# Which ten queries share a block of the attention: neighbours in the score tile, or every twelfth

## The chip, the core and the metric

The kernel runs on one core of a Trainium2 chip. Its time is the device time of one execution in microseconds (us), and a kernel's time is the median over its runs. The core has TensorE (PE in the profile, with its weight loads as PEld), VectorE (DVE), ScalarE (ACT), GpSimd (POOL) and SyncE (SP). SP computes nothing here; it issues nearly all transfers, which 16 DMA engines carry out.

## What is computed

The reference is an attention with mixed heads, followed by a mixture of experts of which each token takes one:

```python
scores = scale * np.matmul(q, k.transpose(0, 1, 3, 2))    # q, k, v: (8, 12, 448, 64)
scores = np.einsum('bhij,hg->bgij', scores, w_pre)        # the 12 heads are mixed
scores = scores - np.max(scores, axis=-1, keepdims=True)
attn = np.exp(scores)
attn = attn / (np.sum(attn, axis=-1, keepdims=True) + 1e-09)
attn = np.einsum('bhij,hg->bgij', attn, w_post)           # and mixed again
attn_out = np.matmul(attn, v)
...
x = np.ascontiguousarray(attn_out.transpose(0, 2, 1, 3)).reshape(B * S, H * D)   # 3584 x 768
expert_idx = np.argmax(x @ w_gate, axis=1)                # one of 8 experts for each token
h = np.maximum(xe @ w1[e], 0.0)
out[mask] = gate_w[mask, None] * (h @ w2[e])
```

## The kernel before

**Tiles.** Each of the 8 batches has 448 queries, cut into four tiles of 120, 120, 120 and 88 queries; so there are 32 tiles T. For a tile, `qk` (L187) multiplies queries by keys, two heads at a time, into PSUM with the query on the partition; ScalarE and VectorE copy the two heads (L200, L201) into the score tile `si`, which holds [query, head, key]: one partition for a query, 12 x 448 numbers in it. There are two such tiles in turn.

**Blocks and halves.** Mixing the heads is a matmul that contracts over the heads, so the heads have to lie on partitions. A tile's queries are therefore cut into blocks of 20, and a block into two halves of 10: `geom[T][3]` (L50 to L55) lists the sizes of the halves. A tile of 120 has 6 blocks; a tile of 88 has 4 blocks and one that is a single half of 8. `relayout` (L207) moves a half by one DMA from 10 partitions of `si` to 120 partitions of a buffer `sb`, row 4 + 12 i + h for query i and head h, 448 numbers (1792 bytes) for each. There are four buffers `sb`, each with room for two halves. Both DMAs of a block are issued from SP at L212.

**Work on a block.** `mix` (L215) multiplies each half by a block-diagonal 124 x 124 matrix (L222, into `bm`), takes the row maximum on VectorE (L223) and the exponential with its sum on ScalarE (L224, into `et`). `weigh` (L229) makes the reciprocal of the sums and scales the second mixing matrix with it on GpSimd (L237, into `wp`). `post` (L241) multiplies `et` by `wp`, which mixes the heads again and turns the block so that keys lie on partitions (L248, into `bp`), and copies each half into the tile `pt` [112 keys, 4, head, 120 queries] at the places of its queries (L254: the first half on ScalarE, the second on VectorE). `av` (L258) multiplies by the values (L267), `rows` (L274), `choose` and `dispatch` send a token's row to HBM (XD) and place it in its expert's list.

**The order.** The attention's order is written out by hand (L416 to L434) and every engine keeps to it. For block u it is: the two DMAs of `relayout` of block u + 2, then `mix` of u, `post` of u - 2, `weigh` of u, then what the table `after` has for that block. For a tile's third block (slot 2) this is `values` of the tile before and `scores` (the six `qk`) of the tile after. So between the last score of the next tile and the first `mix` of that tile lie blocks 3, 4, 5 of a tile with six blocks, but block 3 and the half block 4 of a tile with five. SP takes its DMAs strictly in this order: the queries' loads (L100, two DMAs, at a tile's last but one block), the keys' loads (L84), the values' load (L115) and the stores of XD (L288) stand between the relayouts. A DMA into `sb` waits until the `mix` that read that buffer is done; the first of a tile waits for the last copy into `si`.

**After the attention** come the experts (L446 to L582), matmuls over weights that are loaded and split as they go, and a loop for the rest, which the change does not touch.

Of the kernel before, what the change touches and what calls it, by code (L numbers as in the profile page):

```python
# [19 lines left out]
B, H, S, D = 8, 12, 448, 64  # L20
# [5 lines left out]
IB = 10  # L26
NB = 2 * IB
IQ = 5
R0, R1 = 4, 124
# [11 lines left out]
def attn_moe_kernel(ctx, tc, qT, kT, v, w_pre, w_post, w_gate, w1, w2, out):  # L41
    nc = tc.nc
# [4 lines left out]
    XD = dram.tile([NT, HD], F32, name="XD")  # L47
    TB = dram.tile([ROWS, 2], F32, name="TB")

    geom = []  # L50
    for T in range(NTILE):
        it = T % 4
        ni = min(IT, S - it * IT)
        geom.append((T // 4, it, ni, [[min(IB, ni - i) for i in range(s, min(s + NB, ni), IB)]
                                      for s in range(0, ni, NB)]))  # L55


    kq = ctx.enter_context(ExitStack())
# [19 lines left out]
    KR, KK, QR, QQ, VV, SI, SB, EE, PT, XT = ({} for _ in range(10))  # L78
# [14 lines left out]
        KK[b, c] = (kh, kl)  # L93

    def load_q(T):
        b, it, ni, _ = geom[T]
        qr = q_p.tile([P, NPAIR, IT], F32, name="qr")
        src = qT[b, :, H * it * IT:H * (it * IT + ni)].rearrange("d (c t i) -> t d c i", c=NPAIR, t=2)
        for half in range(2):
            nc.sync.dma_start(out=qr[half * D:(half + 1) * D, :, :ni], in_=src[half])  # L100
        QR[T] = qr
# [25 lines left out]
    for c in range(4):  # L127
# [19 lines left out]
        out=Wpre[:, R0:].rearrange("p (i g) -> p i g", g=H),  # L147
# [13 lines left out]
    for c in range(NPAIR):  # L161
# [22 lines left out]
                        in_=none.unsqueeze(1).to_broadcast([P, 8, ROWS // P // 8, 2]))  # L184


    def qk(T, c):  # L187
        b, it, ni, _ = geom[T]
        if c == 0:
            SI[T] = si_p.tile([IT, H, S], F32, name="si")  # L190
        kh, kl = KK[b, c]
        qh, ql = QQ[T]

        bs = bank_s[c % 2]
        for n, (qx, kx) in enumerate(((qh, kh), (qh, kl), (ql, kh))):
            for r in range(2):
                hs = slice(r * D, (r + 1) * D)
                nc.tensor.matmul(out=bs[:ni, r, :S], lhsT=qx[hs, c, :ni], rhs=kx[hs, :],  # L198
                                 start=(n == 0), stop=(n == 2))
        nc.scalar.copy(out=SI[T][:ni, 2 * c, :], in_=bs[:ni, 0, :S])  # L200
        nc.vector.tensor_copy(out=SI[T][:ni, 2 * c + 1, :], in_=bs[:ni, 1, :S])  # L201
# [5 lines left out]
    def relayout(T, s):  # L207
        sb = sbs[nsb["n"] % len(sbs)]
        nsb["n"] += 1
        for c, nq in enumerate(geom[T][3][s]):  # L210
            q0 = s * NB + c * IB
            nc.sync.dma_start(out=sb[R0:R0 + nq * H, c, :], in_=SI[T][q0:q0 + nq])  # L212
        SB[T, s] = sb

    def mix(T, s):  # L215
# [25 lines left out]
    def post(T, s):  # L241
        if s == 0:
            PT[T] = pt_p.tile([JC, NJ, H, IT], F32, name="pt")
        et, wp = EE.pop((T, s))
        for n, nq in enumerate(geom[T][3][s]):
            pp = bank_p[n]
            for c in range(NJ):
                nc.tensor.matmul(out=pp[:, c * IT:(c + 1) * IT],  # L248
                                 lhsT=et[:R1, n, c * JC:(c + 1) * JC],
                                 rhs=wp[:R1, n, :], start=True, stop=True)  # L250
        for n, nq in enumerate(geom[T][3][s]):
            i0 = s * NB + n * IB
            copy = (nc.scalar.copy, nc.vector.tensor_copy)[n]
            copy(out=PT[T][:, :, :, i0:i0 + nq].rearrange("p c h i -> p (c h) i"),  # L254
                 in_=bank_p[n][:, :NJ * IT].rearrange("p (x i) -> p x i", i=IB)[:, :, :nq])


    def av(T, g):  # L258
        b, it, ni, _ = geom[T]
        if g == 0:  # L260
            XT[T] = x_p.tile([P, NPAIR, IT], F32, name="xt")
        pa = bank_s[g][:, 0, :3 * IT].rearrange("p (c i) -> p c i", i=IT)
        for p in range(3):
            for c in range(NJ):
                for r in range(2):
                    h = 2 * (3 * g + p) + r
                    nc.tensor.matmul(out=pa[r * D:(r + 1) * D, p, :ni],  # L267
                                     lhsT=VV[b][:, c, h * D:(h + 1) * D],
                                     rhs=PT[T][:, c, h, :ni], start=(c == 0), stop=(c == NJ - 1))
        nc.vector.tensor_copy(out=XT[T][:, 3 * g:3 * g + 3, :ni], in_=pa[:, :, :ni])  # L270
# [1 line left out]
    XR, LG = {}, {}  # L272

    def rows(T, part):  # L274
        b, it, ni, _ = geom[T]
        if part == 0:
            XR[T] = x_p.tile([IT, NPAIR, P], F32, name="xr", bufs=1)
            LG[T] = sm_p.tile([IT, 2, NE], F32, name="lg")
        pxv = bank_s[part][:, 0, :3 * XG].rearrange("p (c x) -> p c x", x=XG)
        for c in range(3):  # L280
            nc.tensor.matmul(out=pxv[:ni, c, :], lhsT=XT[T][:, part * 3 + c, :ni],
                             rhs=xg[:, part * 3 + c, :], start=True, stop=True)
        nc.scalar.copy(out=XR[T][:ni, part * 3:part * 3 + 3, :], in_=pxv[:ni, :, :P])
        nc.vector.reduce_sum(out=LG[T][:ni, part, :],
                             in_=pxv[:ni, :, P:XG].rearrange("p c e -> p e c"), axis=AX.X)
        if part == 1:
            t0 = b * S + it * IT
            nc.sync.dma_start(out=XD[t0:t0 + ni, :],  # L288
                              in_=XR.pop(T)[:ni].rearrange("p c x -> p (c x)"))
# [2 lines left out]


    def choose(T):
        b, it, ni, _ = geom[T]
        lg2 = LG.pop(T)
        lg = sm_p.tile([IT, NE], F32, name="lgs")
        nc.vector.tensor_add(out=lg[:ni], in0=lg2[:ni, 0, :], in1=lg2[:ni, 1, :])
        m8 = sm_p.tile([IT, NE], F32, name="m8")
        i8 = sm_p.tile([IT, NE], U32, name="i8")  # L300
        nc.vector.max(out=m8[:ni], in_=lg[:ni])
        nc.vector.max_index(out=i8[:ni], in_max=m8[:ni], in_values=lg[:ni])
        sc = sm_p.tile([IT, 4], F32, name="sc")
        nc.vector.tensor_copy(out=sc[:ni, 0:1], in_=i8[:ni, 0:1])
        ohb = sm_p.tile([IT, NE], BF16, name="ohb")
        nc.vector.tensor_scalar(out=ohb[:ni], in0=iota8[:ni], scalar1=sc[:ni, 0:1], scalar2=None,
                                op0=ALU.is_equal)
        nc.vector.tensor_scalar(out=sc[:ni, 1:2], in0=m8[:ni, 0:1], scalar1=-1.0, scalar2=None,
                                op0=ALU.mult)
        ex = sm_p.tile([IT, NE], F32, name="ex")  # L310
        nc.scalar.activation(out=ex[:ni], in_=lg[:ni], func=AF.Exp, bias=sc[:ni, 1:2],
                             scale=1.0, accum_out=sc[:ni, 2:3])
        LG[T] = (sc, ohb)

    def dispatch(T):
        b, it, ni, _ = geom[T]
        sc, ohb = LG.pop(T)
        pr = bank_s[0][:, 1, :]
        nc.tensor.matmul(out=pr[:ni, 0:NE], lhsT=tri[:ni, :ni], rhs=ohb[:ni], start=True, stop=True)
        nc.tensor.matmul(out=pr[:, NE:2 * NE], lhsT=ones[:ni, :], rhs=ohb[:ni], start=True, stop=True)  # L320
        nc.vector.tensor_scalar(out=sc[:ni, 2:3], in0=sc[:ni, 2:3], scalar1=1e-9, scalar2=None,
                                op0=ALU.add)
        tg = sm_p.tile([IT, 2], F32, name="tg")
        nc.vector.reciprocal(out=tg[:ni, 1:2], in_=sc[:ni, 2:3])
        nc.vector.tensor_copy(out=tg[:ni, 0:1].bitcast(I32), in_=tokid[:ni, b, it:it + 1])
        pos = sm_p.tile([IT, NE], F32, name="pos")
        nc.vector.tensor_tensor(out=pos[:ni], in0=pr[:ni, 0:NE], in1=state["base"][:ni], op=ALU.add)
        nc.vector.tensor_tensor(out=pos[:ni], in0=pos[:ni], in1=ohb[:ni], op=ALU.mult)
        di = sm_p.tile([IT, 1], I32, name="di")
        nc.vector.reduce_sum(out=sc[:ni, 3:4], in_=pos[:ni], axis=AX.X)  # L330
        nc.vector.tensor_copy(out=di[:ni], in_=sc[:ni, 3:4])
        nc.gpsimd.indirect_dma_start(
            out=TB[:, :], out_offset=bass.IndirectOffsetOnAxis(ap=di[:ni, 0:1], axis=0),
            in_=tg[:ni, :], in_offset=None, bounds_check=ROWS - 1, oob_is_err=False)
        last = T == NTILE - 1
        nbase = (const if last else sm_p).tile([P, NE], F32, name="cbase" if last else "nbase")
        nc.vector.tensor_tensor(out=nbase, in0=pr[:, NE:2 * NE], in1=state["base"], op=ALU.add)
        state["base"] = nbase
# [38 lines left out]
        after.setdefault((T, s), []).append(what)  # L377

    for T in range(NTILE):
        b, it, ni, _ = geom[T]  # L380
        n = len(geom[T][3])
        last = T + 1 == NTILE
        if T + 2 < NTILE:
# [32 lines left out]
    for u in range(NU + PLAG):  # L416
# [6 lines left out]
        if u < NU:  # L423
# [3 lines left out]
            T, s = blocks[u]  # L427
# [7 lines left out]
    T = NTILE - 1  # L435
# [264 lines left out]
```

## Time and profile before

| what | value |
|---|---|
| median of 3 runs | 1793.27 us (1791.68 to 1803.64) |
| the profiled execution | 1798.46 us, span from first to last instruction 1796.7 us |
| attention, from the first score to the last token's row | about 7 to 1225 us of the span |
| experts | about 1225 to 1785 us |
| mean granted clock of TensorE over the span | 0.956 |
| L212 issues on SP, `sb<-si` | 352 DMAs of 210.0 KB and 8 of 168.0 KB |

How to read it: the page of the profile gives busy times by engine, then the costliest groups of instructions by line, with the idle time of the engine just before them and what ended that idle time (the releaser). The view of waits sums such idle times. The view of stretches gives each engine's busy time between two moments, the granted clock of TensorE (1.00 is full speed) and the share of the 16 DMA engines that was busy. The view of DMA queues gives packets, bytes and the share of the 16 engines' time that the packets took. In the timeline each row has the start in us, the duration, the engine, the line, the operation, output and inputs, the count, and in brackets the idle time before and its releaser.

### The profile page before, as it was taken

Reading aid. Unit: us, or ns where it says so; the run is one execution under the profiler, and the core shown is the slowest. Engines: PE = TensorE matmul, PEld = TensorE weight load, DVE = VectorE, ACT = ScalarE, POOL = GpSimd, SP = SyncE. Lnnn points to the kernel's source line nnn. Section 1 sums busy time; section 2 is a strip of 40 time slices with the busy share of each in tenths; the row PEclk is TensorE's granted clock in tenths of the full one; section 3 lists DMA queues with packets and bytes.
Section 4 is the critical chain, followed back from the end, with each engine's and each line's share of the span. In section 5 each row is a group of like instructions: output and inputs, shape, how many; then the busy total and the mean of one; then the engine's idle time right before and its main releaser. Section 6 shows DMA issues by size and latency. Waiting matters only on the chain. (4 is left out here: it accounts for less than half of the span.)

```text
span 1796.7 us, 29795 instructions
## 1 busy us (share of the span) xinstructions
PE 1538.0 (86%) x11056; PEld 1233.2 (69%) x11056; DVE 812.7 (45%) x2011; ACT 703.3 (39%) x1608; POOL 428.0 (24%) x595
## 2 busy tenths in 40 slices
PE   3788788788789788888879889965999999999996
PEld 1566566566566566666657666655988889898986
DVE  1455454455455545545445545543334333344330
ACT  2344444345345444444434544532324233234230
POOL 4224223123222322323312422212102102011000
PEclk9899999899899999989999999987999999999998
DMA  3554455355455455445535544444335244154220
GB/s 87 138 108 81 98 127 103 75 117 127 78 122 107 90 110 122 81 98 132 107 75 121 126 82 85 94 109 139 127 117 186 87 148 161 59 197 170 85 90 33
DMA packets 114468, 197.53 MB, mean 110 GB/s; under 512 B 39746, under 2 KB 88914, under 8 KB 114308
## 3 DMA queue, kind: packets, MB, share of 16 engines
q1 hardware_dynamic: 107200, 171.51, 40.1%
q0 software_dynamic: 6064, 23.86, 3.5%
q8 instruction: 100, 1.64, 0.4%
q14 instruction: 60, 0.49, 0.1%
q10 hardware_dynamic: 1044, 0.04, 0.0%
HBM read 96.01 MB, written 23.06 MB: 66 GB/s over the span
## 5 line engine op out<-in xcount | busy, mean ns | idle before, releaser
L222 PE MATMUL bm<-sb,Wpre 124*124 124x448 f32 x720 | 350.4, 596 | 150.8 <-DMA sb<-si 114.8
L248 PEld LDWEIGHTS bp<-wp,et 124*112 124x112 f32 x2880 | 349.4, 189 | 87.6 <-issue 84.2
L237 POOL TENSOR_SCALAR wp<-Wpost,st 124x120 f32<-124x120 f32 x360 | 206.2, 584 | 831.4 <-DVE st L234 733.7
L248 PE MATMUL bp<-wp,et 124*112 124x120 f32 x2880 | 350.5, 278 | 6.6 <-ACT pt L254 6.6
L224 ACT ACTIVATE et<-bm,st 124x448 f32<-124x448 f32 x360 | 226.5, 632 | 330.9 <-DVE st L223 330.9
L222 PEld LDWEIGHTS bm<-sb,Wpre 124*124 124x124 f32 x720 | 121.4, 197 | 263.1 <-issue 134.9
L223 DVE TENSOR_REDUCE st<-bm 124x1 f32<-124x448 f32 x360 | 218.3, 620 | 172.6 <-PE bm L222 154.8
L200 ACT COPY si<-bs 120x448 f32<-120x448 f32 (+1 forms) x192 | 102.1, 532 | 254.9 <-PE bs L198 253.1
L254 DVE COPY pt<-bp 112x480 f32<-112x480 f32 x176 | 115.6, 657 | 158.0 <-PE bp L248 141.7
L201 DVE COPY si<-bs 120x448 f32<-120x448 f32 (+1 forms) x192 | 119.4, 623 | 101.3 <-ACT si L200 93.1
L267 PE MATMUL bs<-pt,vt 112*64 112x120 f32 (+1 forms) x3072 | 156.7, 263 | 0.6 <-ACT pt L254 0.6
L267 PEld LDWEIGHTS bs<-pt,vt 112*64 112x64 f32 x3072 | 149.8, 139 | 4.6 <-ACT pt L254 0.9
L528 PE MATMUL pm_h<-xh,ah 128*128 128x512 f32 (+1 forms) x384 | 147.4, 384 | 4.5 <-DVE hl L532 2.9
L528 PE MATMUL pm_h<-xl,ah 128*128 128x512 f32 (+1 forms) x384 | 146.6, 382 | 0.0
L528 PE MATMUL pm_h<-xh,al 128*128 128x512 f32 (+1 forms) x384 | 146.5, 382 | 0.0
L556 POOL DMA_INDIRECT out<-y,ti x30 | 33.6, 1121 | 463.7 <-ACT xh L483 346.5
L198 PE MATMUL bs<-kh,qh 64*120 64x448 f32 (+1 forms) x384 | 87.0, 449 | 50.4 <-DVE si L201 37.5
L547 PE MATMUL pm_y<-bh,hh 128*128 128x384 f32 x480 | 127.9, 343 | 0.0
L547 PE MATMUL pm_y<-bl,hh 128*128 128x384 f32 x480 | 126.0, 336 | 0.0
L547 PE MATMUL pm_y<-bh,hl 128*128 128x384 f32 x480 | 122.4, 336 | 0.0
L254 ACT COPY pt<-bp 112x480 f32<-112x480 f32 (+1 forms) x184 | 103.0, 560 | 5.9 <-PE bp L248 5.8
L198 PEld LDWEIGHTS bs<-kh,qh 64*120 64x120 f32 (+1 forms) x384 | 33.8, 172 | 101.2 <-DVE si L201 72.4
(100 smaller groups left out, 1820.8 us busy)
## 6 DMA issues: line engine op xcount, KB each, us to landing
sb<-si SPq DMA_DIRECT2D x352, 210.0 KB
wraw<-in_w SPq DMA_DIRECT2D x48, 512.0 KB
wraw<-in_w SPq DMA_DIRECT2D x64, 384.0 KB
kr<-in_kT SPq DMA_DIRECT2D x48, 224.0 KB
vt<-in_v SPq DMA_DIRECT2D x8, 1344.0 KB
qr<-in_qT SPq DMA_DIRECT2D x48, 180.0 KB
XD<-xr SPq DMA_DIRECT2D x24, 360.0 KB
qr<-in_qT SPq DMA_DIRECT2D x16, 132.0 KB
```

What stands on the lines that cost most here:

```text
L198: nc.tensor.matmul(out=bs[:ni, r, :S], lhsT=qx[hs, c, :ni], rhs=kx[hs, :], start=(n == 0), stop=(n == 2))
L200: nc.scalar.copy(out=SI[T][:ni, 2 * c, :], in_=bs[:ni, 0, :S])
L201: nc.vector.tensor_copy(out=SI[T][:ni, 2 * c + 1, :], in_=bs[:ni, 1, :S])
L222: nc.tensor.matmul(out=bm, lhsT=Wpre[:R1, :], rhs=sb[:R1, c, :], start=True, stop=True)
L223: nc.vector.reduce_max(out=st[:R1, 0, c:c + 1], in_=bm, axis=AX.X, negate=True)
L224: nc.scalar.activation(out=et[:R1, c, :], in_=bm, func=AF.Exp, bias=st[:R1, 0, c:c + 1], scale=1.0, accum_out=st[:R1, 1, c:c + 1])
L237: nc.gpsimd.tensor_scalar(out=wp[:R1, c, :], in0=Wpost[:R1], scalar1=st[:R1, 2, c:c + 1], scalar2=None, op0=ALU.mult)
L248: nc.tensor.matmul(out=pp[:, c * IT:(c + 1) * IT], lhsT=et[:R1, n, c * JC:(c + 1) * JC], rhs=wp[:R1, n, :], start=True, stop=True)
L254: copy(out=PT[T][:, :, :, i0:i0 + nq].rearrange("p c h i -> p (c h) i"), in_=bank_p[n][:, :NJ * IT].rearrange("p (x i) -> p x i", i=IB)[:, ...
L267: nc.tensor.matmul(out=pa[r * D:(r + 1) * D, p, :ni], lhsT=VV[b][:, c, h * D:(h + 1) * D], rhs=PT[T][:, c, h, :ni], start=(c == 0), stop=( ...
L528: nc.tensor.matmul(out=ph[:, :n], lhsT=wx[:, fs], rhs=xx[:, kt, :n], start=(m == 0), stop=(m == 3 * NK1 - 1))
L547: nc.tensor.matmul(out=py[g][:, :384], lhsT=hx[:, kt, ts], rhs=wx[:, g * 384:(g + 1) * 384], start=(n == 0), stop=(n == 3 * NK2 - 1))
```

## The change

The halves of a tile are formed in another way. With N the number of halves of the tile (12 for 120 queries, 9 for 88), half n now takes the queries n, n + N, n + 2N and so on, not ten neighbours. The function `queries` gives this slice. It is used in two places: as the partitions of `si` that a relayout's DMA reads, and as the places in `pt` where the copies of `post` write. The score tile, the buffer `sb`, all matmuls and the order of the work stay. In a tile of 88 the halves are now seven of 10 and two of 9, where they were eight of 10 and one of 8.

```diff
         ni = min(IT, S - it * IT)
-        geom.append((T // 4, it, ni, [[min(IB, ni - i) for i in range(s, min(s + NB, ni), IB)]
-                                      for s in range(0, ni, NB)]))
+        N = -(-ni // IB)
+        halves = [-(-(ni - n) // N) for n in range(N)]
+        geom.append((T // 4, it, ni, [halves[n:n + 2] for n in range(0, N, 2)], N))
+
+    def queries(T, s, c):
+        N, n = geom[T][4], 2 * s + c
+        return slice(n, n + N * (geom[T][3][s][c] - 1) + 1, N)
...
         for c, nq in enumerate(geom[T][3][s]):
-            q0 = s * NB + c * IB
-            nc.sync.dma_start(out=sb[R0:R0 + nq * H, c, :], in_=SI[T][q0:q0 + nq])
+            nc.sync.dma_start(out=sb[R0:R0 + nq * H, c, :], in_=SI[T][queries(T, s, c)])
...
         for n, nq in enumerate(geom[T][3][s]):
-            i0 = s * NB + n * IB
             copy = (nc.scalar.copy, nc.vector.tensor_copy)[n]
-            copy(out=PT[T][:, :, :, i0:i0 + nq].rearrange("p c h i -> p (c h) i"),
+            copy(out=PT[T][:, :, :, queries(T, s, n)].rearrange("p c h i -> p (c h) i"),
                  in_=bank_p[n][:, :NJ * IT].rearrange("p (x i) -> p x i", i=IB)[:, :, :nq])
```

The remaining lines of the diff unpack the tuple with `geom[T][:3]`. No instruction changes its place on any engine; what changes is the form of some. On SP, around the first tile of 88 queries (the names are buffers and their sources; x2 is two DMAs in a row), before:

```order
L212 DMA sb_139<-si 120x1x448 x2
L212 DMA sb_140<-si 120x1x448 x2
L212 DMA sb_141<-si 96x1x448
L212 DMA sb_142<-si 120x1x448 x2
L100 DMA qr<-in_qT 64x6x120 x2
L212 DMA sb_139<-si 120x1x448 x2
L288 DMA XD<-xr 120x768
L212 DMA sb_140<-si 120x1x448 x2
```

And with the change, at the same place:

```order
L219 DMA sb_139<-si 120x1x448 x2
L219 DMA sb_140<-si 120x1x448
L219 DMA sb_140<-si 108x1x448
L219 DMA sb_141<-si 108x1x448
L219 DMA sb_142<-si 120x1x448 x2
L108 DMA qr<-in_qT 64x6x120 x2
L219 DMA sb_139<-si 120x1x448 x2
L294 DMA XD<-xr 120x768
L219 DMA sb_140<-si 120x1x448 x2
```

Only the sizes of the last two halves differ: 108 and 108 rows stand where 120 and 96 stood. The first `sb` of the next tile still stands ahead of the two loads of `qr`, and the second one behind them.

More of the change, by code (lines that the diff above doesn't have):

```diff
@@ L95, in load_q @@
     def load_q(T):
-        b, it, ni, _ = geom[T]
+        b, it, ni = geom[T][:3]
         qr = q_p.tile([P, NPAIR, IT], F32, name="qr")
@@ L187, in qk @@
     def qk(T, c):
-        b, it, ni, _ = geom[T]
+        b, it, ni = geom[T][:3]
         if c == 0:
@@ L251, in post @@
         for n, nq in enumerate(geom[T][3][s]):
-            i0 = s * NB + n * IB
             copy = (nc.scalar.copy, nc.vector.tensor_copy)[n]
-            copy(out=PT[T][:, :, :, i0:i0 + nq].rearrange("p c h i -> p (c h) i"),
+            copy(out=PT[T][:, :, :, queries(T, s, n)].rearrange("p c h i -> p (c h) i"),
                  in_=bank_p[n][:, :NJ * IT].rearrange("p (x i) -> p x i", i=IB)[:, :, :nq])
     def av(T, g):
-        b, it, ni, _ = geom[T]
+        b, it, ni = geom[T][:3]
         if g == 0:
@@ L274, in rows @@
     def rows(T, part):
-        b, it, ni, _ = geom[T]
+        b, it, ni = geom[T][:3]
         if part == 0:
@@ L294, in choose @@
     def choose(T):
-        b, it, ni, _ = geom[T]
+        b, it, ni = geom[T][:3]
         lg2 = LG.pop(T)
@@ L315, in dispatch @@
     def dispatch(T):
-        b, it, ni, _ = geom[T]
+        b, it, ni = geom[T][:3]
         sc, ohb = LG.pop(T)
@@ L379, in attn_moe_kernel @@
     for T in range(NTILE):
-        b, it, ni, _ = geom[T]
+        b, it, ni = geom[T][:3]
         n = len(geom[T][3])
```

## The prediction

> **What bounds the kernel now.** I read the page first, for the engine that is busiest and for what it waits.
>
> ```profile
> span 1796.7 us, 29795 instructions
> PE 1538.0 (86%) x11056; PEld 1233.2 (69%) x11056; DVE 812.7 (45%) x2011; ACT 703.3 (39%) x1608; POOL 428.0 (24%) x595
> L222 PE MATMUL bm<-sb,Wpre 124*124 124x448 f32 x720 | 350.4, 596 | 150.8 <-DMA sb<-si 114.8
> sb<-si SPq DMA_DIRECT2D x352, 210.0 KB
> ...
> L222 PE MATMUL bm<-sb,Wpre x720: 537/539/1110, 35.1 to 1197.8; 124*124 124x448 f32 x180
> ```
>
> TensorE is busy 86% of the span, and its one large idle time stands ahead of L222, the first matmul on a half: 114.8 us of waits for the relayout's DMA, which is the transfer that the change touches. The last row, the line by itself, has the least, middle and greatest duration of that matmul: 539 ns is its usual one, the mean of 596 has slow ones in it, up to twice as long. Next I took the waits of TensorE in the even part of the attention, from the first score matmul of the second tile (55.9) to that of the last (1150.1), and the busy times of the same stretch, of a six-block interval and of the five-block ones. An interval runs from a tile's first score matmul to the next tile's; it holds six blocks, or four and a half where a tile of 88 ends in it. There are 30 of them, 7 of the short kind.
>
> ```profile
> PE bm L222 <- DMA sb<-si: 99.0, 75, 3.1
> PE bs L198 <- DVE si L201: 36.3, 60, 0.7
> PE bm L222 <- ACT et L224: 21.5, 22, 1.7
> ...
> core 0: us, PE busy (x) PEld busy (x) DVE busy (x) ACT busy (x) POOL busy (x), PEclk, DMA share, GB/s
> 55.90:1150.10 1094.20, 931.72 (x7759) 698.12 (x7758) 562.69 (x1586) 490.59 (x1249) 323.38 (x472) 0.95 0.49 104
> 643.40:678.40 35.00, 30.92 (x270) 23.57 (x266) 19.31 (x55) 16.33 (x42) 9.73 (x15) 1.00 0.53 119
> ...
> 165.10:202.50 37.40, 28.53 (x238) 21.07 (x236) 16.31 (x48) 14.17 (x35) 8.07 (x12) 0.91 0.43 83
> 1044.90:1079.70 34.80, 28.00 (x238) 20.23 (x236) 16.29 (x48) 13.95 (x35) 8.07 (x12) 0.90 0.43 86
> sum 257.70, PE 199.31 PEld 145.25 DVE 114.10 ACT 98.84 POOL 56.49; mean PE 28.47 PEld 20.75 DVE 16.30 ACT 14.12 POOL 8.07
> ```
>
> Three things are to be seen. Of 1094.2 us, TensorE is idle 162.5, and 99.0 of these are the relayout. The other engines are busy for half of an interval, so TensorE and the DMA bound it. And the clock is 1.00 in the interval with few waits but 0.90 in the short ones: idle time is paid twice, once as idle and once as a slower clock behind it. The last row sums the seven short intervals (165.1 is the first, 1044.9 the last): 36.8 us each. The other 23 share 1094.2 - 257.7 = 836.5, which is 36.4 each.
>
> Then the transfer itself. At the start nothing else is in its way: the first rows are TensorE's timeline, the next SP's; behind them stand the packets of the SP's queue (q1) in three stretches, and the SP row that belongs to the third.
>
> ```profile
> 35.09 1.86 PE L222 MATMUL bm<-sb,Wpre 124*124 124x448 f32 x2 [6.79 <-DMA sb<-si]
> 38.05 3.35 PE L222 MATMUL bm<-sb,Wpre 124*124 124x448 f32 x4 [1.10 <-DMA sb<-si]
> 41.94 0.99 PE L222 MATMUL bm<-sb,Wpre 124*124 124x448 f32 x2 [0.54 <-DMA sb<-si]
> 50.30 3.32 PE L222 MATMUL bm<-sb,Wpre 124*124 124x448 f32 x4 [7.37 <-DMA sb<-si]
> ...
> 29.56 7.48 SPq L212 DMA_DIRECT2D sb<-si  x4
> ...
> q1 hardware_dynamic: 59, 0.11, 54.0%
> ...
> q1 hardware_dynamic: 144, 0.23, 31.7%
> ...
> q1 hardware_dynamic: 199, 0.33, 50.2%
> ...
> 813.97 20.12 SPq L212 DMA_DIRECT2D sb<-si  x8
> ```
>
> The first half is issued at 29.56 and used at 35.09, 5.53 us later; the second half is used 2.96 us after the first. The first q1 row is 31.0 to 32.5, when only these halves move: 54.0% of 16 engines for 1.5 us is 12.96 us, over 59 packets 220 ns each. The second is 13.5 to 16.0, when one load of keys moves packets of the same 1792 bytes into 128 partitions: 31.7% of 40 us over 144 is 88 ns. The third is 827 to 829, when nothing is left in the queue but halves issued before: 50.2% of 32 us over 199 is 81 ns. So a relayout's packet can go in 81 ns and takes 220 when ten engines start together on ten neighbouring partitions. The writes go to 120 partitions, as spread as the keys' are; what is close together is the reading side. The change spreads just that.
>
> **The transfer, part by part.** A half of 120 packets, ten at a time, is 12 packets in a row: 12 x 0.220 = 2.64 us by the mean, 2.96 by the pace of the halves. Spread out I take the keys' row, 12 x 0.088 = 1.06 us; the bounds are 2.96 (the reading side was not it) and 12 x 0.081 = 0.97. A half then is in place 5.53 - 2.96 + 1.06 = 3.6 us after its issue, and a second one about 0.9 us after it, since SP issues no faster. [...]
>
> **What that saves.** A block without a wait is seen here, in a six-block interval:
>
> ```profile
> 803.57 1.67 PE L222 MATMUL bm<-sb,Wpre 124*124 124x448 f32 x4
> 805.07 1.80 PE L248 MATMUL bp<-wp,et 124*112 124x120 f32 x16
> 807.02 1.77 PE L222 MATMUL bm<-sb,Wpre 124*124 124x448 f32 x4
> ```
>
> It takes 3.45 us, less than the two halves' 5.9 us of transfer, and more than the 2.1 that they would need. The floor of a six-block interval is the 30.92 busy at full clock plus 36.3 / 30 = 1.2 of score copies: 32.1. For a short one, clock 0.90 over 34.8 us is 3.5 us of lost clock; at its busy share of 0.80 that is 2.8 of the 28.00, so 25.2 + 1.2 = 26.4. What stays on top of the floor is seen in the short interval's own rows, TensorE's and SP's:
>
> ```profile
> 620.23 0.92 PE L222 MATMUL bm<-sb,Wpre 124*124 124x448 f32 x2
> 623.02 1.02 PE L222 MATMUL bm<-sb,Wpre 124*124 124x448 f32 x2 [1.87 <-DMA sb<-si]
> 623.87 1.80 PE L248 MATMUL bp<-wp,et 124*112 124x120 f32 x16
> 627.70 1.13 PE L222 MATMUL bm<-sb,Wpre 124*124 124x448 f32 x2 [2.00 <-DMA sb<-si]
> 631.47 1.82 PE L222 MATMUL bm<-sb,Wpre 124*124 124x448 f32 x2 [2.64 <-DMA sb<-si]
> ...
> 614.53 1.64 SPq L212 DMA_DIRECT2D sb<-si  x2
> 616.26 5.65 SPq L100 DMA_DIRECT2D qr<-in_qT  x2
> 622.00 1.72 SPq L212 DMA_DIRECT2D sb<-si  x2
> 623.82 2.53 SPq L288 DMA_DIRECT2D XD<-xr  x1
> ```
>
> The new tile's first block is issued at 614.5 and 615.4 and would land by 619.0, ahead of its use at 620.2: the 1.87 go. The second block stands on SP behind the two loads of queries, which hold SP for 5.65 us; issued at 622.0, it lands at 625.6. TensorE, no longer held before, is ready at 620.2 + 1.67 + 1.64 + 0.2 = 623.7, so a wait of 1.9 us stays where 2.00 and 2.64 stood. The third block, behind XD, lands in time. Short intervals keep 2.0 of DMA and, I take, 1.0 of exponentials and clock: 26.4 + 3.0 = 29.4, a gain of 7.4 x 7 = 52. In a long interval the second block has another block and a half of cover, so no DMA wait stays; I leave 1.0 for the exponential (21.5 / 30 = 0.7 now, and blocks that come faster meet it sooner): 33.1, a gain of 3.3 x 23 = 76. At the start the third block waits behind the values' load (50.30); two earlier blocks whose pace falls from 2.96 to about 1 us a half bring it forward by about 7. The experts and the end are not touched: 0.
>
> **The copies into pt.** L254 will write 4 bytes every 48, where it wrote runs of 40 bytes.
>
> ```profile
> L254 DVE COPY pt<-bp x176: 640/658/660, 56.0 to 1209.7; 112x480 f32<-112x480 f32 x176
> L201 DVE COPY si<-bs x192: 620/624/626, 11.1 to 1156.5; 120x448 f32<-120x448 f32 x144, 88x448 f32<-88x448 f32 x48
> L223 DVE TENSOR_REDUCE st<-bm 124x1 f32<-124x448 f32 x360 | 218.3, 620 | 172.6 <-PE bm L222 154.8
> ...
> 807.62 0.17 DVE L232 TENSOR_SCALAR st<-st 124x2 f32<-124x2 f32 x1
> 807.82 0.17 DVE L234 RECIPROCAL st<-st 124x2 f32<-124x2 f32 x1
> ```
>
> Today's breaks after every tenth number cost nothing: 658 ns for 480 against 624 for 448 without breaks is 1.06 ns a number. No row has a write with such a step, so below it is 0 and above I take a doubling, 0.5 us a copy. VectorE's block is 2 x 0.62 + 0.66 + 0.34 = 2.24 of 3.45 us; 0.5 more still fits, but in the two blocks with the routing's small operations it could cost a wait of 1 us a tile, 32 in all. I take 0. This holds 32 us for the range.
>
> **The sum.** 52 + 76 + 7 = 135. Against the profiled execution's 1798.5 this is 1663; against the median of the runs, which lies 5 lower, 1658. I say 1660.
>
> **The rivals.** First, the wait stays with SP: faster halves don't help where the issue is late, and the short intervals keep all they have. For it: 5.65 us of query loads ahead of the second block. Against it: those halves are used 5.7 us after the issue at 622.0, of which the transfer is the larger part. It would cost the 52 again: 1712.
>
> Second, TensorE's clock stays low although the waits shrink. Clock 0.95 over 1094.2 us loses 54.7, at a busy share of 0.85 some 46 us: 1706. Against it stands the 1.00 of the interval 643.4, with waits still in it.
>
> Third, the change does not do what it is about: ten engines with 12 packets each set the pace wherever the partitions lie, and halves still come 2.96 us apart: 1793, no change. For it: the number of packets, engines and bytes stays. Against it: 81 ns in the third stretch, of the same packets.
>
> Fourth, it is slower: the write with a step of 48 bytes makes the copy of L254 the longest work of a block. With c for VectorE's copy a block takes 1.24 + 0.34 + 0.2 between instructions + c; it passes 3.45 at c = 1.7, and eats the 135 us over 180 blocks (0.75 each) at c = 2.4, which is 4.7 ns a number in place of 1.06. At 6 ns, c = 3.0 and the block 4.8: 1660 + 180 x 1.35 = 1903. No row speaks for a factor over 4. [...]
>
> **Chances.** Forecast 0.77, SP 0.08, clock 0.06, no change 0.05, slower copies 0.04. A measurement of this kernel tells about 1% from no change, so faster has 0.91, same 0.05, slower 0.04. The likeliest case has its own range from 1638 (half of the 44 us that I leave above the floors, 23 + 21, gone too) to 1692 (the 32 us of copies). The range goes from 1638 to 1708, so that the clock's case is in it.
>
> **What would show it.** Right: the wait of L222 for `sb<-si` falls from 114.8 to 20 to 40 us, most of it in the short intervals and the start; the mean of L222 falls from 596 towards the 539; the mean clock rises above 0.97; long intervals take 33 us, short ones 29.5; L254 stays at 0.66 us on VectorE and the experts keep their time. Wrong: packets still at 220 ns when a half goes alone; L254 above 1.2 us; or short intervals above 34 us with the wait still on the relayout.

## The result, and the profile after

The changed kernel takes 1635.16 us (median of 4 runs, 1631.32 to 1637.5) where the kernel before took 1793.58 beside it: 0.910 of its time, with a 95% interval from 0.907 to 0.914. That is 158 us less. The prediction had 1660 and a range from 1638: right in direction and cause, and 25 us too slow, so the measured time lies just below the range.

The page of the changed kernel, with the lines that answer to those of before (L229 is the old L222, L260 the old L254):

```profile
span 1634.6 us, 29795 instructions
PE 1491.6 (91%) x11056; PEld 1208.6 (74%) x11056; DVE 860.4 (53%) x2011; ACT 767.2 (47%) x1608; POOL 429.4 (26%) x595
...
L229 PE MATMUL bm<-sb,Wpre 124*124 124x448 f32 x720 | 316.6, 562 | 32.3 <-ACT et L231 19.2
L260 DVE COPY pt<-bp 112x480 f32<-112x480 f32 (+1 forms) x176 | 179.0, 1017 | 129.8 <-PE bp L255 121.8
L260 ACT COPY pt<-bp 112x480 f32<-112x480 f32 (+1 forms) x184 | 186.3, 1013 | 2.3 <-PE bp L255 2.3
```

The idle time ahead of the first matmul on a half fell from 150.8 to 32.3 us, and the relayout is no longer its main releaser. VectorE and ScalarE are busier, since the copies into `pt` take 1017 and 1013 ns where they took 657 and 560. The waits of TensorE between the first score of the second tile and the first score of the last (now 49.3 to 982.7):

```profile
PE bs L206 <- DVE si L209: 36.3, 60, 0.7
PE bm L229 <- ACT et L231: 13.3, 14, 1.2
PE bm L229 <- DMA sb<-si: 0.8, 1, 0.8
```

Of 99.0 us of waits for the relayout 0.8 are left. The same stretch by busy times, then one long interval, then the first of the seven short intervals and their sum:

```profile
core 0: us, PE busy (x) PEld busy (x) DVE busy (x) ACT busy (x) POOL busy (x), PEclk, DMA share, GB/s
49.30:982.70 933.40, 879.25 (x7757) 668.40 (x7756) 607.90 (x1586) 550.03 (x1249) 323.70 (x472) 1.00 0.39 122
...
545.00:577.20 32.20, 30.59 (x272) 23.60 (x268) 20.75 (x55) 18.64 (x42) 9.73 (x15) 1.00 0.47 143
...
144.70:171.60 26.90, 24.81 (x240) 18.74 (x238) 17.27 (x48) 15.58 (x35) 8.07 (x12) 1.00 0.38 125
...
sum 188.30, PE 173.67 PEld 131.26 DVE 120.84 ACT 109.04 POOL 56.52; mean PE 24.81 PEld 18.75 DVE 17.26 ACT 15.58 POOL 8.07
```

The clock is 1.00 throughout this stretch, where it was 0.95. TensorE is busy 94% of the stretch, which took 1094.2 us and takes 933.4. Short intervals take 26.9 us (36.8 before), long ones (933.4 - 188.3) / 23 = 32.4 (36.4 before). The packets of the lone first halves, 31.0 to 32.5, are in the view of DMA queues:

```profile
q1 hardware_dynamic: 191, 0.32, 57.3%
```

That is 57.3% of 24 us (16 engines for 1.5 us) over 191 packets, 72 ns each, where it was 220. Ten of the 191 are of 4 bytes and take 9 ns; the other 181, each a row of 1792 bytes, take 75 on the mean. The 59 packets before were all such rows. TensorE's and SP's timeline at the start and in a short interval (642.6 to 669.5):

```profile
32.49 6.52 PE L229 MATMUL bm<-sb,Wpre 124*124 124x448 f32 x8 [4.21 <-DMA sb<-si]
43.12 3.32 PE L229 MATMUL bm<-sb,Wpre 124*124 124x448 f32 x4 [4.11 <-DMA sb<-si]
...
655.44 1.67 PE L229 MATMUL bm<-sb,Wpre 124*124 124x448 f32 x4
658.93 1.77 PE L229 MATMUL bm<-sb,Wpre 124*124 124x448 f32 x4
662.38 1.77 PE L229 MATMUL bm<-sb,Wpre 124*124 124x448 f32 x4 [0.78 <-ACT et L231]
```

```profile
29.54 3.50 SPq L219 DMA_DIRECT2D sb<-si  x4
...
649.74 1.67 SPq L219 DMA_DIRECT2D sb<-si  x2
651.50 1.35 SPq L108 DMA_DIRECT2D qr<-in_qT  x2
652.94 1.72 SPq L219 DMA_DIRECT2D sb<-si  x2
```

The first half is used 2.95 us after its issue (5.53 before), and four halves in a row feed eight matmuls without a gap. In the short interval, blocks follow each other every 3.45 us. Look at the row of the queries' loads: the two hold SP for 1.35 us, where the same two DMAs held it for 5.65.

The span is 162.1 us shorter: 160.8 in the stretch and 6.6 ahead of it, less 5.3 behind it. Of these 5.3, 0.6 lie before the experts' first transpose (85.5 us after the stretch before, 86.1 now) and 4.7 in the experts themselves (561.1 us before, 565.8 now), whose code is the same. In the ten profiled executions below, with the same code there, the experts took 561.3 to 569.8 us, so the 4.7 lie within their spread.

### The profile page after: what moved, and what is told of

Same layout as the page of the kernel before. It is cut to its first block, busy times and chain, and to the rows that moved or that the text cites. A ratio compares the mean times of both kernels' runs of the same rounds, so it can differ in the third digit from the quotient of the medians.

```text
span 1634.6 us, 29795 instructions
## 1 busy us (share of the span) xinstructions
PE 1491.6 (91%) x11056; PEld 1208.6 (74%) x11056; DVE 860.4 (53%) x2011; ACT 767.2 (47%) x1608; POOL 429.4 (26%) x595
## 5 line engine op out<-in xcount | busy, mean ns | idle before, releaser
L255 PEld LDWEIGHTS bp<-wp,et 124*112 124x112 f32 x2880 | 321.1, 178 | 88.8 <-issue 85.0
L229 PE MATMUL bm<-sb,Wpre 124*124 124x448 f32 x720 | 316.6, 562 | 32.3 <-ACT et L231 19.2
L255 PE MATMUL bp<-wp,et 124*112 124x120 f32 x2880 | 332.1, 269 | 8.1 <-ACT pt L260 8.1
L260 DVE COPY pt<-bp 112x480 f32<-112x480 f32 (+1 forms) x176 | 179.0, 1017 | 129.8 <-PE bp L255 121.8
L230 DVE TENSOR_REDUCE st<-bm 124x1 f32<-124x448 f32 x360 | 213.0, 618 | 15.9 <-PE bm L229 11.5
L229 PEld LDWEIGHTS bm<-sb,Wpre 124*124 124x124 f32 x720 | 121.5, 189 | 122.4 <-ACT et L231 52.6
L260 ACT COPY pt<-bp 112x480 f32<-112x480 f32 (+1 forms) x184 | 186.3, 1013 | 2.3 <-PE bp L255 2.3
L538 DVE SCALAR_TENSOR_TENSOR hl<-pm_h,hh 128x512 fp32r<-128x512 f32 (+1 forms) x64 | 42.0, 657 | 126.6 <-ACT hh L537 126.6
```

The costliest lines, as they stand in the source:

```text
L229: nc.tensor.matmul(out=bm, lhsT=Wpre[:R1, :], rhs=sb[:R1, c, :], start=True, stop=True)
L230: nc.vector.reduce_max(out=st[:R1, 0, c:c + 1], in_=bm, axis=AX.X, negate=True)
L255: nc.tensor.matmul(out=pp[:, c * IT:(c + 1) * IT], lhsT=et[:R1, n, c * JC:(c + 1) * JC], rhs=wp[:R1, n, :], start=True, stop=True)
L260: copy(out=PT[T][:, :, :, queries(T, s, n)].rearrange("p c h i -> p (c h) i"), in_=bank_p[n][:, :NJ * IT].rearrange("p (x i) -> p x i", i= ...
```

## The experiments

The theory after the result: the relayout's reading side was the bottleneck, since a row takes 220 ns when a half is read from ten neighbouring partitions and 75 when it is read from every twelfth; the copies pay for their step but hide; and the prediction left too much on top of the floor since it took SP's 5.65 us for SP's own work. The rivals: the copies are on the path, the halves' new sizes matter, or any gap between partitions is as good as twelve.

**Step one part alone: the copies.** The DMA reads neighbours again, the copies keep the new places (`places`, added above these lines, gives the run of neighbours):

```diff
-            nc.sync.dma_start(out=sb[R0:R0 + nq * H, c, :], in_=SI[T][queries(T, s, c)])
+            nc.sync.dma_start(out=sb[R0:R0 + nq * H, c, :], in_=SI[T][places(T, s, c)])
```

> The copies into pt write every twelfth place as in the changed kernel, but the relayout reads ten neighbouring partitions as before (the tokens come out in another order, the amount of work is the same). Theory: copies at 1013 to 1017 ns, relayout packets at 220 ns when a half goes alone, and no gain: 1793 to 1815 us, the copies being hidden or costing up to 20. Rival: the gain comes from something else that the change does, as its halves of 9 and 10 queries in the short tiles; then 1700 us or less.

Measured: 1799.88 us (10 runs), 1.002 of before (0.999 to 1.004). (This kernel does the same work but leaves each tile's tokens in another order.) Its packets from 31.0 to 32.5, its wait and its copies:

```profile
q1 hardware_dynamic: 57, 0.10, 52.4%
```

```profile
PE bm L234 <- DMA sb<-si: 109.6, 80, 8.3
```

```profile
L265 DVE COPY pt<-bp 112x480 f32<-112x480 f32 (+1 forms) x176 | 178.3, 1013 | 156.8 <-PE bp L260 141.2
```

The packets are back: 52.4% of 24 us over 57 is 221 ns, and the wait is 109.6 us. The halves of 9 and 10 are in this kernel too, so they are not the cause. While the relayout is the bound, the longer copies cost at most 0.4%, the upper end of the interval.

**The other part alone: spread reads with short copies.** The host lays out a tile's queries so that half n holds ten neighbouring queries although it lies on every twelfth partition of the score tile; `pt` is then written in runs of ten:

```diff
-            copy(out=PT[T][:, :, :, queries(T, s, n)].rearrange("p c h i -> p (c h) i"),
+            copy(out=PT[T][:, :, :, places(T, s, n)].rearrange("p c h i -> p (c h) i"),
...
+    def order(ni):
+        N = -(-ni // IB)
+        column = [n + N * i for n in range(N) for i in range(-(-(ni - n) // N))]
+        return _np.argsort(column)
...
-            inputs["q"][:, :, i:i + IT].transpose(0, 3, 1, 2).reshape(B, D, -1)
+            inputs["q"][:, :, i:i + IT][:, :, order(min(IT, S - i))].transpose(0, 3, 1, 2).reshape(B, D, -1)
```

> The host lays the queries of each tile in another order, so that half n of a tile holds ten neighbouring queries and yet lies on every twelfth partition of the score tile: the relayout reads as in the changed kernel, and the copies into pt write runs of ten as in the kernel before. Theory: the whole gain comes from the relayout's reading side, and the longer copies of the changed kernel (1013 to 1017 ns) lie beside other work; so copies of 560 and 657 ns again, relayout packets as in the changed kernel, and 1635 us within 6. Rival: the longer copies delay the maximum and the exponential behind them, which shows as the 19.2 us for which TensorE waits for the exponential; then those waits shrink by 10 us or more and the time is 1615 to 1625 us.

Measured: 1625.0 us (1621.79 to 1631.91, 5 runs), 0.906 of before (0.903 to 0.908). Neither expectation holds as written: the time is below the theory's 1629 to 1641 and at the upper end of the rival's 1615 to 1625, but the waits for the exponential did not shrink (18.9 us against 19.2), so the rival's mechanism is not it. It was run again beside the changed kernel on one chip:

> The changed kernel once more, to stand beside the next one on the same chip: 1635 us within 6.

> The kernel with queries laid out by the host and short copies into pt, on the same chip as the changed kernel. In the first run it was at 1625 us against 1635, and its profile gives 0.2 to 0.4 us less in a long interval and some 5 us less behind the last score, where ScalarE has the weights' splits and the copies. Theory: the longer copies of the changed kernel do cost, 6 us by the 23 long intervals and 5 at the end: 8 to 14 us faster than the changed kernel. Rival: the two kernels are the same and the difference was the chip: within 4 us of it.

Measured: 1635.56 us (1633.93 to 1637.64, 6 runs) for the changed kernel and 1627.51 (1623.33 to 1631.38, 6 runs) for the other, 8 us less, with no run of the one among the runs of the other. This is the version that beats both kernels; the host's work on the order of the queries is not in the device time. Where the 8 us are is seen in the first start of the experts' transposes, the first number behind the durations, for the changed kernel twice and the other twice:

```profile
L487 PE MATMUL pm_x<-ident,xs x192: 270/273/476, 1068.8 to 1537.0; 128*128 128x128 f32 x192
```

```profile
L487 PE MATMUL pm_x<-ident,xs x192: 270/273/477, 1068.3 to 1534.6; 128*128 128x128 f32 x192
```

```profile
L492 PE MATMUL pm_x<-ident,xs x192: 270/273/477, 1058.6 to 1524.1; 128*128 128x128 f32 x192
```

```profile
L492 PE MATMUL pm_x<-ident,xs x192: 270/273/477, 1059.8 to 1532.0; 128*128 128x128 f32 x192
```

The attention ends 8.5 to 10 us sooner. Two thirds of that come from the long intervals, which take 31.9 to 32.8 us with short copies and 32.1 to 33.2 with long ones (but for the first, 29.9 with either); 2 to 3 us come behind the last score, where 5 were expected and where ScalarE splits weights as well. So the copies' step costs the changed kernel 8 to 10 us. How it reaches TensorE is not shown: in the stretch, the waits that the profile counts differ by only 1.6 us. The two engines spend (1013 - 564) x 184 ns and (1017 - 655) x 176 ns more on copying, 83 and 64 us, and nearly all of that hides behind TensorE.

**How far apart is far enough.** In the tiles of 120 the step between a half's partitions was made 2, 3 and 4 (step 2 is shown):

```diff
         N, n = geom[T][4], 2 * s + c
+        if N == IB + 2:
+            first = n // 2 * 2 * IB + n % 2
+            return slice(first, first + 2 * (IB - 1) + 1, 2)
```

> In the tiles of 120 a half takes every second partition (0, 2, ... 18 and 1, 3, ... 19); the tiles of 88 stay as in the changed kernel. [...] Rival: only neighbours collide, any gap is enough: packets at 75 to 90 ns.

> In the tiles of 120 a half takes every third partition (0, 3, ... 27). [...]

> [...]

Measured: 1647.37 us (1643.89 to 1651.41) with step 2, 1638.94 (one run) with step 3, 1641.26 (1638.75 to 1642.38) with step 4. The packets of the lone first halves, and the copies on VectorE (least, middle and greatest; those of the tiles of 88, whose step is 9, are in it), for step 2, 3 and 4:

```profile
q1 hardware_dynamic: 94, 0.17, 55.1%
```

```profile
L263 DVE COPY pt<-bp x176: 642/659/1064, 54.4 to 1053.4; 112x480 f32<-112x480 f32 x168, 112x432 f32<-112x432 f32 x8
```

```profile
q1 hardware_dynamic: 129, 0.22, 53.7%
```

```profile
L263 DVE COPY pt<-bp x176: 760/858/1073, 52.6 to 1039.5; 112x480 f32<-112x480 f32 x168, 112x432 f32<-112x432 f32 x8
```

```profile
q1 hardware_dynamic: 153, 0.26, 55.3%
```

```profile
L263 DVE COPY pt<-bp x176: 919/1046/1084, 54.6 to 1048.8; 112x480 f32<-112x480 f32 x168, 112x432 f32<-112x432 f32 x8
```

By share times 24 us over the count, packets take 141 ns with step 2, 100 with step 3 and 87 with step 4, against 72 with step 12 and 220 with neighbours; without the packets of 4 bytes the rows take 141, 103 and 90, against 75 and 220. So a gap alone is not enough: for step 2 the rival has 75 to 90 ns, and the rows take 141.

The single packets of the same 1.5 us, which the trace keeps, say more. About ten rows are under way at a time, with neighbours as with step 12, and their times gather at 74, 141 and 267 ns:

| partitions of a half | rows | under 110 ns | 110 to 200 | above 200 |
|---|---|---|---|---|
| step 12 | 181 | 177 | 4 | 0 |
| step 4 | 147 | 114 | 33 | 0 |
| step 3 | 125 | 72 | 53 | 0 |
| step 2 | 94 | 4 | 90 | 0 |
| ten neighbours | 59 | 2 | 19 | 38 |

Rows times the usual time of their column say how many of the ten go at which pace, an estimate from the counts and the three times alone: with step 12, 9.6 at 74 ns and 0.4 at 141; with step 4, 6.4 and 3.6; with step 3, 4.2 and 5.8; with step 2, 0.2 and 9.8; with ten neighbours 0.1, 2.1 and, at 267 ns, 7.8. So over these five, the closer together the ten partitions lie, the more of the ten reads are slow, and the slower. Which partition a packet came from is not in the trace, so which partitions slow each other is not shown. At 141 ns two halves take 2 x 12 x 0.141 = 3.4 us, no more than a block's 3.45, so the time of the kernel changes little: TensorE's waits for the relayout over the whole span are 26.9, 15.1 and 16.7 us, against 9.1 with step 12.

The copies' step: 8 bytes from one write to the next cost nothing (659 ns on VectorE against 657 for runs of 40 bytes), 12 bytes cost 0.20 us (858) and 16 bytes 0.39 (1046), about what 48 bytes cost (1019). With step 3 the halves are also of two kinds. On VectorE the two halves that begin at a place in `pt` which is a multiple of four (32 and 92) take 771 and 776 ns on the mean and the other four 846 to 869; on ScalarE (0 and 60) it is 763 and 774 against 845 to 854. So where a half begins counts as well as its step; why is not shown.

**Who holds SP.** Only the halves of a tile's first block are spread; the other ten are runs of neighbours between them, and the tiles of 88 are cut as in the kernel before:

```diff
-        halves = [-(-(ni - n) // N) for n in range(N)]
+        halves = [min(IB, ni - i) for i in range(0, ni, IB)]
...
         N, n = geom[T][4], 2 * s + c
+        if N == IB + 2 and s:
+            first = N * (n - 2) + 2
+            return slice(first, first + IB)
+        if N < IB + 2:
+            return slice(n * IB, n * IB + geom[T][3][s][c])
```

> Only the two halves of a tile's first block are spread: partitions 0, 12, ... 108 and 1, 13, ... 109 in the tiles of 120. The other ten halves are the runs of ten between them, 2 to 11, 14 to 23 and so on, and the tiles of 88 are as before. The question is why the two loads of queries hold SP for 5.65 us behind a tile's first block. Theory: the load itself costs SP 0.65 each, as in the changed kernel, and the rest is the backlog of the two slow halves issued just before; so with these two spread the loads take 1.3 us together although all other halves are slow, the second block is issued 4 us sooner, and the time is 1690 to 1740 us. Rival, which the prediction assumed: SP needs 5.65 us for loads cut so small, whatever lies before them; then they take 5 us or more, only the first block's wait goes, and the time is 1765 to 1785 us.

Measured: 1770.11 us (1766.6 to 1776.88), 0.987 of before (0.981 to 0.992). SP and TensorE in a short interval of this kernel, and its wait over the span:

```profile
591.75 1.65 SPq L224 DMA_DIRECT2D sb<-si  x2
593.48 1.34 SPq L113 DMA_DIRECT2D qr<-in_qT  x2
594.92 1.72 SPq L224 DMA_DIRECT2D sb<-si  x2
```

```profile
597.45 1.67 PE L234 MATMUL bm<-sb,Wpre 124*124 124x448 f32 x4
600.94 1.02 PE L234 MATMUL bm<-sb,Wpre 124*124 124x448 f32 x2
603.91 0.99 PE L234 MATMUL bm<-sb,Wpre 124*124 124x448 f32 x2 [1.96 <-DMA sb<-si]
```

```profile
PE bm L234 <- DMA sb<-si: 91.9, 74, 8.1
```

Each theory is right in one half. SP: the two loads of queries take 1.34 us when the two halves issued just before them are spread, so most of the 5.65 before was the backlog of two slow halves. The run has its own control: behind a first block of a tile of 88, whose halves are not spread, the pair takes 5.23 to 5.71 us (seven times), and behind every spread one 1.34 to 1.36. The trace of the kernel before had a pair without backlog too, the very first one. These are one pair of this run behind a tile of 88, and the first pair of the kernel before:

```profile
130.24 5.71 SPq L113 DMA_DIRECT2D qr<-in_qT  x2
```

```profile
0.80 1.43 SPq L100 DMA_DIRECT2D qr<-in_qT  x2
```

Time: it fell by 23 us, as the rival said, not by the 53 to 103 that I expected. A slow half issued 4 us sooner is still a slow half: the second half of the second block is waited for as before, and 91.9 us of waits are left. Freeing SP is little without faster halves.

**The hold put back.** The opposite test: the changed kernel with SP held on purpose, by two or three small loads into one scratch tile, each of which waits for the one before (two are shown, without the line that makes the tile):

```diff
         QR[T] = qr
+        if T > 1:
+            for _ in range(2):
+                nc.sync.dma_start(out=hold, in_=src[0, :, 0, :88])
```

> The changed kernel with two small loads more behind each tile's loads of queries, both into one scratch tile that nothing reads, so that SP waits for the first to land before it issues the second. That holds SP some 3.3 us longer between a tile's first and second block. The prediction left 2.0 us of waits in each short interval because it took SP to be held 5.65 us there; in the changed kernel it is held 1.35 and the wait is gone. Theory: the wait was reckoned rightly and only the hold was wrong, so with the hold put back the wait is back: SP held about 4.7 us, the second block's halves issued 3.3 us later, 0.5 to 1.2 us of wait for the relayout in each of the 8 short stretches, and 1638 to 1646 us. Rival: something else covers it, no wait comes back, 1635 us within 4.

> The same with three such loads, which hold SP some 6 us longer than in the changed kernel, 7.5 in all. Theory: 3 to 3.7 us of wait for the relayout in each of the 8 short stretches, 0 to 1 in the long intervals, in all 1655 to 1675 us. Rival: no wait comes back, 1635 us within 4.

Measured: 1639.77 us (1636.06 to 1642.53) with two and 1661.22 (1659.65 to 1663.32) with three. SP and the wait in one short interval, with two and then with three:

```profile
657.46 1.38 SPq L109 DMA_DIRECT2D qr<-in_qT  x2
658.89 3.32 SPq L113 DMA_DIRECT2D hold<-in_qT  x2
662.31 1.76 SPq L223 DMA_DIRECT2D sb<-si  x2
```

```profile
PE bm L233 <- DMA sb<-si: 0.9, 2, 0.5
```

```profile
671.33 1.38 SPq L109 DMA_DIRECT2D qr<-in_qT  x2
672.76 5.28 SPq L113 DMA_DIRECT2D hold<-in_qT  x3
678.13 1.76 SPq L223 DMA_DIRECT2D sb<-si  x2
```

```profile
PE bm L233 <- DMA sb<-si: 3.2, 2, 2.7
```

Held 4.7 us, SP brings 0.9 us of wait back in this interval; held 6.7 us, 3.2. Over the whole span the waits for the relayout rise from 9.1 to 21.5 and 36.0 us. Between the two rows, a hold of 5.65 us would cost 2.0 us here, as the prediction reckoned. This interval is one of the milder: the seven short ones are longer than in the changed kernel by 1.6 us on the mean with two loads and 3.9 with three, which makes about 2.7 for 5.65. So the prediction's reckoning of what such a hold costs was about right; that the hold would be there was wrong.

## Why the prediction came out as it did

- **What bounds the kernel, and the transfer.** Right, and for the stated reason. The packets take 72 ns; the keys' row gave 88 and the bound 81, so the transfer came out below its lower bound. Those two rows were read as means of rows of 1792 bytes, but 16 and 17 of their packets are of 4 bytes (without them 98 and 87 ns), and a few take much longer: 110 of the keys' 128 rows are under 110 ns, most of them at 74, and the other 18 pull the mean up. A half is in place 2.95 us after its issue where 3.6 stood.
- **The floors.** Right: 32.1 and 26.4 were forecast as what an interval takes with no waits and a full clock, and the intervals now take 32.4 and 26.9. They were a little high: they hold 23 x 30.92 + 7 x 25.2 = 887.6 us of TensorE's work, and TensorE is busy 879.3.
- **What stays on top of the floors: this step failed.** The prediction left 2.0 + 1.0 us in each short interval and 1.0 in each long one, 44 us in all. Measured are 933.4 - (23 x 32.1 + 7 x 26.4) = 10.3 us. In the short intervals it said that the second block "stands on SP behind the two loads of queries, which hold SP for 5.65 us". These 5.65 us were read from the profile as the cost of the loads, but most of them were the queue's backlog of the halves that the change speeds up: in the changed kernel the loads take 1.35, and the second block is issued 3.2 us after the first where it was 7.5. So the 2.0 us of DMA vanished too; the short intervals gained 69 us in place of 52. The 1.0 for exponentials was a guess upward from 0.7; it went down to 13.3 / 30 = 0.4, and the clock lost nothing. The long intervals gained 91 in place of 76.
- **The start** gained 6.6 us for 7.
- **The copies into pt.** The longer copy, held only as a bound of 0.5 us more, is what happened: 0.36 us more on VectorE (1.02), 0.45 more on ScalarE (1.01). Of the signs given for the forecast, that L254 stays at 0.66 us failed. It cost 8 to 10 us, inside the 0 to 32 of the range, where the sum took 0.
- **The sum.** 160.8 + 6.6 - 5.3 for 135. Without the 7 x 2.0 us that were put down to SP the forecast would have been 1646, inside its own range; the 0.6 us too much for the exponential in each of 30 intervals is another 18. Against these stand the experts' 4.7. What the copies cost lies for the most part inside the measured intervals.
- **The rivals.** SP stays the wait: excluded for the changed kernel, and shown as possible by the held ones. Clock stays low: it is 1.00. No change: excluded. Slower copies decide: at 1.06 + 360 / 480 = 1.8 ns a number on VectorE, far from the 4.7 at which they would.
- **The range** began at half of the 44 us, because the guess of what stays was treated as a thing that might halve, not as a thing that hangs on one number, the 5.65, which could fall to nothing.

Still open: what makes the experts, whose code is the same, take between 561.1 and 569.8 us, how the longer copies make the long intervals longer, and which partitions slow each other's reads.

## What to carry to other kernels

When a transfer's packets are slow although its engines are busy, compare packets of the same size elsewhere in the same trace; here rows of 1792 bytes took 220 ns on the mean from ten neighbouring partitions and 75 from every twelfth, so it was worth choosing which partitions one DMA reads at a time. Time that SP spends on an issue is not the cost of that issue alone: behind slow transfers it had their backlog in it, and went away with them (5.65 us for the two loads of queries, then 1.35), so a residual wait should be reckoned with the issue time of an unloaded stretch. When an order of elements has to be changed for the sake of a transfer, put the permutation where it costs the kernel nothing, here in the layout of an operand, and keep the strided write out of the engines' copies (8 us here).

## What the runs showed of the hardware that was not expected

A pair of loads of 180 KB each, in pieces of 480 bytes, holds SP for 1.35 us when the halves before it move fast, and for 5.65 us when they move slowly. Rows of 1792 bytes, read from ten partitions at a time, gather at 74, 141 and 267 ns: from every twelfth partition 177 of 181 are under 110 ns, from every fourth 114 of 147, from every third 72 of 125, from every second 4 of 94, and from ten neighbours 38 of 59 are above 200. A copy from PSUM that writes 4 bytes every 8 costs what one in runs of 40 bytes does (659 ns against 657), every 12 a third more (858), every 16 or 48 more than half as much again (1046 and 1019).
